# Five changes of order in a gated mix of linear and softmax attention: reciprocals at an iteration's end, weight splits moved, spare banks taken on another turn, the end of the maxima behind its visit, finished sums copied by two engines

## The chip, the cores and the metric

The kernel runs on one core of a Trainium2 chip. The core's engines work side by side: TensorE (PE, with its weight loads shown apart as PEld) multiplies matrices, VectorE (DVE) and ScalarE (ACT) read TensorE's results from the PSUM banks and work element by element, GpSimd (POOL) works from SBUF, and SyncE (SP) issues the transfers (DMA). Every engine runs its own instructions in order and waits on semaphores for the others. The metric is the device time of one execution in microseconds (us); less is better.

## The reference

Two attentions over the same 2048 tokens (448 features, 16 heads of 28) are mixed by a gate per token. Cut to what is computed:

```python
# branch A: linear attention with the Hedgehog feature map
q, k, v = split(x @ A_wqkv)                      # per head: 2048 x 28
phi = lambda u: concat(softmax(u @ w_phi), softmax(-(u @ w_phi)))   # 28 -> 56
kv, z = phi(k).T @ v, phi(k).sum(over tokens)
a = concat_heads((phi(q) @ kv) / (phi(q) @ z + 1e-6)) @ A_wo
# branch B: softmax attention over all keys
q, k, v = split(x @ B_wqkv)
b = concat_heads(softmax(q @ k.T * 28**-0.5) @ v) @ B_wo
g = sigmoid((x * gate_w).sum(-1))
out = g * a + (1 - g) * b
```

Everything is float32. The kernel keeps that precision with a cheaper matmul type (fp32r): an operand is split into a high part (a cast, mostly on ACT) and a low part (the difference, a subtraction on DVE or GpSimd), and a product is made of three passes, high by high, high by low, low by high.

## The kernel before

The heads go in 4 groups of 4, the tokens in 16 tiles of 128 or in 4 query blocks of 512. The order of the instructions on PE, DVE, ACT and GpSimd is the order in which the program writes them; for SP's queue of transfers a scheduler chooses the order. The program has three loops.

**Loop 1 (n below 20)** projects branch B's queries and keys (`proj_qk`, PSUM tiles `pqk`), which go to HBM (qkd), and splits weights: `split_part` casts one half of a weight at once on ACT and queues the subtraction in a list `lows`; `take_lows()` issues what is in the list on DVE.

**Loop 2 (i below 43; q = i - 16, y = q - 1, tb = y // 2)** is branch A with branch B's value projection behind it. The features of keys and queries are made (`features1`, `features2`), `turn` transposes them (`pft`, copied by ACT to `fT`), and `numer(tb)` multiplies them with the summed keys and values (`pn`, two banks). Such a sum then takes four steps, two tiles tb apart, for 8 blocks named a0 to a7:

- `normalize1` copies the two banks to `oUa` on ACT (L362) and has SP gather the denominators (dena).
- `normalize2` adds 1e-6 and inverts on DVE (L371, L372); SP stores the reciprocals to HBM (rda) and loads them back broadcast over partitions (rsa, L377).
- `normalize3` multiplies `oUa` by `rsa` on DVE (L383).
- `normalize4` splits the product into high and low (`oTa`) for the output projection (`poa`, `out_a`).

In the body of loop 2 `normalize2` of block tb - 2 stands after `normalize3` and ahead of the value projection, the weight splits, `numer`, `turn`, `out_a` and the score units. The weights wvB (branch B's values) are split in two halves, at q 14 and 16; `value_b` (tiles `pvb`) uses them at the end of the loop and after it.

Branch B's softmax needs the maximum of each row of scores ahead of the exponentials. The maxima are worked out over the whole program as filler between other matmuls. In loops 1 and 2 and after them `mx_unit` does it 76 times: four matmuls into two pairs of banks (`pmb`, `pmd`, L267), a relu on ACT (L270) and two reductions on DVE (L272) into `part`. In loop 3 `mx_visit` does the rest: up to three score tiles `pm` (three banks, one buffer, L303) and one large reduction on DVE (L311). When a block of queries is complete, `mx_reduce` puts a function into the list `fin`: three small DVE operations that end the maxima. `mx_fin()` runs them at the start of the next unit or visit, and SP then loads the negated maxima into the query tile `qst`.

**Loop 3 (s below 272)** is the softmax attention. Step s (group and query block s // 16, key tile s % 16) makes two score tiles of two banks each (`scores`, `st`, L795), each followed by an exponential on ACT (L797, tile `p`); then `values(s - 1)` adds p times v into one bank `pv` (L898); then `mx_visit` follows. When 16 key tiles are done, `finish` runs `normalize1` with n = 1: here DVE copies the whole of `pv` to `oUb` (L362), and the other three steps follow 3, 8 and 9 steps later. For the last group of heads the output projection (`project`, `pob`, L912) comes from 10 steps after, one tile a step.

The score tiles take turns on two buffers of two banks (`ps2`). Once the maxima are all visited their three banks are free: two of them become a third score buffer, the spare, and one the bank of `pob`:

```python
def ps_p(nm, last=False):
    if spare and spare[0] is not None and not last:
        turns["n"] += 1
        if turns["n"] % 3 == 1:
            return spare[0].tile([P, 2, 512], F32, tag="p", name=nm, bufs=1)
    return ps2.tile([P, 2, 512], F32, tag="p", name=nm, bufs=2)
```

The last sum is finished apart (`finish_last`), with matmuls of the output projection as filler.

Of the kernel before, what the change touches and what calls it, by code (L numbers as in the profile page):

```python
# [19 lines left out]
D = 448  # L20
# [19 lines left out]
def gated_mix_kernel(ctx, tc, xT, wqkB, wvB, wvA, wkAT, wqAT, phi, woA, woB,  # L40
# [7 lines left out]
    nc = tc.nc  # L48
# [106 lines left out]
    mxs = {"u": 0, "f": 0, "fin": []}  # L155
# [55 lines left out]
    def mx_fin():  # L211
        while mxs["fin"]:
            mxs["fin"].pop(0)()
# [72 lines left out]

    def mx_visit():

        mx_fin()
        f = mxs["f"]  # L290
        todo = flats[f:f + 3]
        todo = [x for i, x in enumerate(todo) if x[4] == todo[0][4] + i]
        if not todo:
            return
        mxs["f"] = f + len(todo)
        pm = psm.tile([P, 3, 512], F32, tag="mx", name=f"pm{f}", bufs=1)
        for i, (gq, kb, qt, j, col) in enumerate(todo):
            g, qb = divmod(gq, NQ)
            if kb == 1 and qt in (0, QM) and j == 0 and gq + 1 < NG * NQ:
                if ("qc", gq + 1) not in mxs:  # L300
                    mx_query(gq + 1)
            js = slice(32 * j, 32 * j + DH)
            nc.tensor.matmul(pm[:, i, :], mxs[("qc", gq)][js, qt * P:(qt + 1) * P],  # L303
                             mxs[("kc", g, kb)][js, :], start=True, stop=True,
                             tile_position=(32 * j, 0))
            if j == 3 and qt == 3 and qb == NQ - 1 and g + 1 < NG:
                mx_load(g + 1, kb)
            if kb == 3 and qt == 3 and j == 3:
                mx_reduce(gq)
        n, col = len(todo), todo[0][4]  # L310
        nc.vector.tensor_reduce(part[:, col:col + n], pm[:, :n], AX.X, ALU.max)  # L311


    bd_s = ExitStack()
# [43 lines left out]
    def normalize1(pool, pn, nm, n):  # L358

        oU = pool.tile([P, n, 512], F32, tag="oU", name=f"oU{nm}", bufs=1 + n)  # L360
        for i in range(n):
            (nc.scalar.copy if n == 2 else nc.vector.tensor_copy)(oU[:, i, :], pn[i])  # L362
        den = pool.tile([P, n, 16], F32, tag="den", name=f"den{nm}", bufs=2)
        for i in range(n):
            nc.sync.dma_start(den[:, i, :], oU[DH:P:32, i, :])
        return oU, den
# [64 lines left out]
    fk, va, fq, fT_of, num, oTs = {}, {}, {}, {}, {}, {}  # L431
# [110 lines left out]
    wvA_s = weights(3, "wvA_s")  # L542
# [19 lines left out]
    def split_part(w, key, n, i, low=nc.vector):  # L562
        split_weight(w, raws[key][i], slice(2 * i, 2 * i + 2), slice(0, n), low)
# [16 lines left out]
    for n in range(NP):  # L580
        take_acts()
        if n in (0, 4, 8):
            x_loads(n // 4 + 1)
        if n == 5:
            nc.sync.dma_start(phi_s, phi)
            load_fold(wkAT, "k")
        if n == 10:
            part_loads("wB1", wqkB[:, :, 512:896], 384, "wB1")
        splits(n + 1)
        if n == 14:  # L590
            part_loads("wvA", wvA, 450, "wvA")
            nc.sync.dma_start(sel_s, sel)
            nc.sync.dma_start(mask_s, mask)
            for v in vap:
                nc.gpsimd.memset(v[:, :, 28:32], 0.0)
                nc.gpsimd.memset(v[:, :, 28:29], 1.0)
        if 16 <= n < 20:
            mx_unit()
        proj_qk(n, ev)
        if n in (17, 18):  # L600
            split_part(wvA_s, "wvA", 450, n - 17)
            take_lows()
        if n == 0:
            pkv = ps_pv("pkv")
        if n in (10, 12, 14, 17):
            fold(wkA_s, "k", {10: 0, 12: 1, 14: 2, 17: 3}[n])
        if n == 10:
            pair_query(0, 0)
            pair_load(0, 0)
        if n == 15:  # L610
            pair_load(0, 1)
            pair_query(0, 1)
        if n in (14, 19):
            take_subs()
# [27 lines left out]
    for i in range(2 * NT + 11):  # L642
        t, q = i, i - NT
        y = q - 1
        tb = y // 2
        take_acts()
        if t < NT and t % 2 == 0:
            mx_unit()
            passes = (55 if t < NT - 4 else 44) + (4 if t >= 4 else 0)
            pace["n"], pace["at"] = 4 if t >= 4 else 0, [k * passes // 4 for k in (1, 2, 3)]  # L650
        if q in (0, 1):
            take_exps()

        if t % 2 == 0 and 0 <= t - 4 < NT:
            kv_add(t - 4)
            kv_add(t - 3)
        if q == 2:
            bk_s.close()
            ta_s = ExitStack()
            ta = ta_s.enter_context(tc.tile_pool(name="ta", bufs=1, reuse_waits="tile"))  # L660
            stg = ta_s.enter_context(tc.tile_pool(name="stg", bufs=2, reuse_waits="tile"))
            KV = ta.tile([112, 8, 64], F32, name="KV")
            kvT = kv_copy()
            ps_s_.close()
            ps = ps_s_.enter_context(tc.tile_pool(name="psq", bufs=1, space=PSUM, reuse_waits="tile"))
            psn[0] = 4
            woA_s = weights(3, "woA_s")
            wvB_s = weights(2, "wvB_s")
            take_exps()
        if t < NT:  # L670
            pk = ps_s(f"pk{t}")
            tok_major(pk, t, wkA_s, D, tick)
            fk[t] = features1(pk, f"k{t}", nc.gpsimd)
            take_exps(1)
        if 0 <= q < NT:
            pq = ps_s(f"pq{q}")
            tok_major(pq, q, wqA_s, D)
        if q == 0:
            fk[NT - 1] = features2(fk[NT - 1], f"k{NT - 1}")
        if q in (1, 2):  # L680
            fq[q - 1] = features2(fq[q - 1], f"q{q - 1}")
        if 0 <= q < NT:
            fq[q] = features1(pq, f"q{q}", nc.vector if 0 < q < 9 else nc.gpsimd)
        if 0 <= t - 1 < NT - 1:
            fk[t - 1] = features2(fk[t - 1], f"k{t - 1}")
        if q in (0, 1) or q >= 8:
            mx_unit()
        if y >= 9 and y % 2 and tb - 4 < 8:
            oTs[tb - 4] = normalize4(ta, num.pop(tb - 4), f"a{tb - 4}", 2)
        if q > 0:  # L690
            take_exps(int(q < NT))
        if q == 3:
            kv_out(kvT)
        if 2 <= q - 1 < NT:
            fq[q - 1] = features2(fq[q - 1], f"q{q - 1}")
        take_subs()
        if t == 1:
            pair_load(0, 3)
        if y >= 8 and y % 2 == 0 and tb - 4 < 8:
            num[tb - 4] = normalize3(*num[tb - 4], 2)  # L700
        if y >= 5 and y % 2 and tb - 2 < 8:
            num[tb - 2] = normalize2(ta, *num[tb - 2], f"a{tb - 2}", 2, True)
        if t < NT:
            value_a(t)
            if t % 2 and t < NT - 4:
                proj_qk(NP + t // 2, ev)
        if q in (0, 1):
            proj_qk(NP + 6 + q, ev)
        take_lows()
        if 2 <= i < 4:  # L710
            fold(wqA_s, "q", i - 2, 0, 2)
            fold(wqA_s, "q", i - 2, 2, 2)
        elif 4 <= i < 6:
            fold(wqA_s, "q", i - 2)
        if q == 1:
            ev_s.close()
        if q == 2:
            part_loads("woA", woA, D, "woA")
        if q == 11:
            part_loads("wvB", wvB, D, "wvB")  # L720
        if q in (4, 6):
            split_part(woA_s, "woA", D, (q - 4) // 2)
        if q in (14, 16):
            split_part(wvB_s, "wvB", D, (q - 14) // 2)
        if q == 1:
            gates()
        if y >= 4 and y % 2 == 0 and tb - 2 < 8:
            numer(tb - 2)
        if y < 9 or y % 2:
            if y >= 2 and y - 2 < NT:  # L730
                turn(y - 2)
        if 0 <= y - 10 < NT:
            out_a(y - 10)
            out_a2(y - 10)
        if y >= 9 and y % 2 == 0 and y - 2 < NT:
            turn(y - 2)
        if NT + 3 <= q < NT + 10:
            mx_unit()
        if q == NT + 2:
            bd_s.close()  # L740
            vb = [value_tile(0)]
        if 0 <= q - NT - 2 < 8:
            value_b(q - NT - 2)
    ta_s.close()
    wp_s.close()
    vb.append(value_tile(1))
# [86 lines left out]
    turns = {"n": 0}  # L833
# [6 lines left out]
    def ps_p(nm, last=False):  # L840
        if spare and spare[0] is not None and not last:
            turns["n"] += 1
            if turns["n"] % 3 == 1:
                return spare[0].tile([P, 2, 512], F32, tag="p", name=nm, bufs=1)
        return ps2.tile([P, 2, 512], F32, tag="p", name=nm, bufs=2)

# [280 lines left out]
```

## Time and profile before

| | us |
|---|---|
| time, median of 3 runs (lowest, highest) | 1064.24 (1063.4, 1065.44) |
| profiled execution, its own time | 1062.24 |
| its span in the trace | 1060.4 |
| PE busy | 1043.4 (98%) |
| ACT busy | 723.3 (68%) |
| DVE busy | 706.6 (67%) |
| PE weight loads busy | 567.0 (53%) |
| GpSimd busy | 227.2 (21%) |

The span runs from the first to the last instruction of the profile; the execution's own time holds 1.8 us around it. A timeline row gives the start in us from the span's start, the mean duration, the engine, the line, the operation, the tiles written and read, their shapes and, behind x, how many like it follow each other; a bracket tells how long the engine had been idle and what it waited for. A row of the list of waits gives the engine that waited, what it wanted to do, whom it waited for, the total, the count and the longest. The granted TensorE clock is 1.0 over the whole span.

### The profile page before, as it was taken

What the parts mean: (1) busy time and instruction counts of PE and PEld (TensorE: products, weight loads), DVE (VectorE), ACT (ScalarE), POOL (GpSimd) and SP (SyncE); (2) the same over time, 40 slices, a digit from 0 to 9 for tenths busy, and PEclk for the clock granted to TensorE, in tenths of its full rate; (3) what the DMA queues carried; (4) which work ended last, traced back from release to release, by engine and by line L of the source; (5) the groups of instructions that cost most, each with busy time, mean ns of one, the idle gap of its engine ahead of it and who ended that gap; (6) DMA issues with size and microseconds to landing.
All of it is one profiled execution on the core that took longest, in us unless ns stands there. A gap on an engine that the chain in (4) does not pass through costs nothing.

```text
span 1060.4 us, 16523 instructions
## 1 busy us (share of the span) xinstructions
PE 1043.4 (98%) x6328; PEld 567.0 (53%) x6328; DVE 706.6 (67%) x871; ACT 723.3 (68%) x864; POOL 227.2 (21%) x188
## 2 busy tenths in 40 slices
PE   7999999999999999999999999999999999999998
PEld 5878777878767634344344344343343343454445
DVE  4666776897745567767677777677677777676302
ACT  4455555577755677887777777777777777747572
POOL 0234454678525600120000000000000000000000
PEclk9999999999999999999999999999999999999999
DMA  8873110122232832232533224432233344142311
GB/s 281 293 237 102 37 42 30 40 68 88 88 102 83 184 78 52 53 76 75 119 73 71 72 61 144 111 69 71 63 69 82 76 111 101 46 123 53 101 58 53
DMA packets 65687, 99.03 MB, mean 93 GB/s; under 512 B 17976, under 2 KB 26792, under 8 KB 65608
## 3 DMA queue, kind: packets, MB, share of 16 engines
q1 hardware_dynamic: 65608, 97.97, 33.8%
q8 instruction: 50, 0.82, 0.3%
q14 instruction: 29, 0.24, 0.1%
HBM read 69.77 MB, written 27.78 MB: 92 GB/s over the span
## 4 chain that ended last, share of the span: by engine, by line
PE 93%; DVE 4%; DMA 1%; ACT 1%; issue 0%; POOL 0%; SPq 0%; DVEq 0%; ACTq 0%
PE st L795 27%; PE pv L898 24%; PE pm L303 10%; PE pqk L108 7%; PE pk L126 4%; PE poa L108 3%; PE pva L126 3%; PE pob L108 3%; PE pmb L267 3%; PE pvb L126 2%; PE pq L108 2%; PE pvb L108 1%; PE pn L496 1%; DMA dena<-oUa 1%; PE pft L484 1%; DVE featq L411 1%
## 5 line engine op out<-in xcount | busy, mean ns | idle before, releaser
L797 ACT ACTIVATE p<-st 128x1024 f32<-128x1024 f32 x512 | 496.5, 1021 | 173.4 <-PE st L795 171.9
L311 DVE TENSOR_REDUCE part<-pm 128x3 f32<-128x1536 f32 (+1 forms) x241 | 421.7, 1750 | 167.7 <-PE pm L303 167.4
L795 PE MATMUL st<-qst,kst 128*128 128x512 f32 x1024 | 306.4, 421 | 1.5 <-DVE part L311 1.5
L898 PE MATMUL pv<-p,vb 128*32 128x512 f32 x2048 | 272.8, 605 | 0.0
L795 PEld LDWEIGHTS st<-qst,kst 128*128 128x128 f32 x1024 | 172.9, 188 | 94.1 <-issue 68.2
L303 PEld LDWEIGHTS pm<-kc,qc 28*128 28x128 f32 x720 | 45.4, 182 | 200.1 <-DVE part L311 184.9
L272 DVE CUSTOM_DVE_ANT_0 rl<-pmb,rl 128x512 f32<-128x512 f32 x152 | 98.1, 683 | 56.9 <-ACT rl L270 56.8
L383 POOL TENSOR_TENSOR oUb<-oUb,rsb 128x512 f32<-128x512 f32 x15 | 19.3, 1286 | 521.2 <-DMA rsb<-rdb 326.0
L303 PE MATMUL pm<-kc,qc 28*128 28x512 f32 x720 | 121.4, 497 | 0.5 <-DVE part L311 0.5
L270 ACT ACTIVATE rl<-pmd 128x1024 f32<-128x1024 f32 x76 | 78.1, 1028 | 42.0 <-PE pmd L267 34.4
L898 PEld LDWEIGHTS pv<-p,vb 128*32 128x32 f32 x2048 | 40.4, 108 | 92.9 <-issue 92.2
L108 PE MATMUL pqk<-XH,wB 128*128 128x512 f32 x224 | 70.9, 407 | 6.7 <-ACT XH L327 6.7
L108 PEld LDWEIGHTS pqk<-XH,wB 128*128 128x128 f32 x224 | 42.1, 193 | 17.4 <-ACT XH L327 6.9
L531 ACT CAST ev<-pqk 128x512 fp32r<-128x512 f32 x28 | 16.4, 586 | 43.0 <-PE pqk L108 39.4
L108 PE MATMUL poa<-woA_s,oTa 128*128 128x448 f32 x192 | 43.4, 375 | 0.0
L267 PE MATMUL pmd<-kp,qp 28*128 28x512 f32 x152 | 37.9, 494 | 3.3 <-DVE part L272 3.3
L126 PE MATMUL pk<-wkA_s,XH 128*128 128x448 f32 x128 | 39.4, 382 | 0.0
L532 DVE TENSOR_TENSOR ev<-pqk,ev 128x512 fp32r<-128x512 f32 x28 | 19.3, 691 | 29.7 <-ACT ev L531 29.6
L108 PEld LDWEIGHTS poa<-woA_s,oTa 128*128 128x128 f32 x192 | 34.9, 189 | 6.2 <-issue 3.3
L267 PE MATMUL pmb<-kp,qp 28*128 28x512 f32 x152 | 38.0, 496 | 0.0
L126 PE MATMUL pva<-wvA_s,XH 128*128 128x450 f32 x128 | 37.8, 371 | 0.0
L108 PE MATMUL pq<-wqA_s,XH 128*128 128x448 f32 x128 | 37.4, 374 | 0.2 <-ACT oUa L362 0.2
(135 smaller groups left out, 1038.9 us busy)
## 6 DMA issues: line engine op xcount, KB each, us to landing
qkd<-ev SPq DMA_DIRECT2D x28, 512.0 KB
qst<-qkd SPq DMA_DIRECT2D x64, 224.0 KB
kst<-qkd SPq DMA_DIRECT2D x64, 224.0 KB
od<-oTb SPq DMA_DIRECT2D x48, 112.0 KB
xraw<-in_xT_dram SPq DMA_DIRECT2D x8, 512.0 KB
rsa<-rda SPq DMA_DIRECT2D x8, 512.0 KB
rsb<-rdb SPq DMA_DIRECT2D x15, 256.0 KB
gad<-ga SPq DMA_DIRECT2D x16, 224.0 KB
```

Of the source, the lines that this page charges most:

```text
L108: nc.tensor.matmul(dst, l, r, start=i == 0, stop=i == len(todo) - 1)
L126: nc.tensor.matmul(dst[:, :n], l, r, start=i == 0, stop=i == len(todo) - 1, skip_group_check=True)
L267: nc.tensor.matmul((pb if j < 2 else pd)[:, j % 2, :], qc[js, qt * P:(qt + 1) * P], kc[js, :], start=True, stop=True, tile_position=(32 * ...
L270: nc.scalar.activation(rl, pd, AF.Relu)
L272: nc.vector.tensor_tensor_reduce(rl[:, i, :], pb[:, i, :], rl[:, i, :], 1.0, LOWEST, ALU.add, ALU.max, part[:, col + i:col + i + 1])
L303: nc.tensor.matmul(pm[:, i, :], mxs[("qc", gq)][js, qt * P:(qt + 1) * P], mxs[("kc", g, kb)][js, :], start=True, stop=True, tile_position= ...
L311: nc.vector.tensor_reduce(part[:, col:col + n], pm[:, :n], AX.X, ALU.max)
L383: (nc.gpsimd if n == 1 else nc.vector).tensor_mul(oU, oU, rs)
L532: nc.vector.tensor_sub(e[:, 1, :], pq, f32(e[:, 0, :]))
L795: nc.tensor.matmul(st[:, jl, :], kst_of[(g, kt // 4)][:, j, (kt % 4) * P:(kt % 4 + 1) * P], qst_of[gq][:, j, :], start=True, stop=True)
L797: nc.scalar.activation(p, st, AF.Exp, scale=SCALE)
L898: nc.tensor.matmul(pv[32 * j:32 * j + 32, :], vb[kt // 8][:, kt % 8, 4 * g + j, :], pt[j // 2][:, j % 2, :], start=kt == 0, stop=kt == NT ...
```

## The change

It has five parts.

1. In loop 2 `normalize2` moves from the middle of the iteration to its end, behind value projection, weight splits, `numer`, `turn`, `out_a`, the late score units and `value_b`.
2. The first half of wvA is split at n = 16 instead of 17 (the second stays at 18), and the second half of wvB at q = 17 instead of 16 (the first stays at 14).
3. The score tiles take the spare banks on every third turn as before, but the first of them is the third score tile behind the opening instead of the first.
4. `mx_visit` takes the functions of `fin` out of the list at its start and runs them behind its own large reduction instead of ahead of its matmuls.
5. In `normalize1` with n = 1 DVE copies columns 0 to 383 of `pv`, and ACT copies columns 384 to 511. With n = 2 ACT copies both banks as before.

```diff
     def mx_visit():
-        mx_fin()
+        fins = mxs["fin"][:]
+        mxs["fin"].clear()
         f = mxs["f"]
         todo = flats[f:f + 3]
         todo = [x for i, x in enumerate(todo) if x[4] == todo[0][4] + i]
         if not todo:
+            for fn in fins:
+                fn()
             return
...
         nc.vector.tensor_reduce(part[:, col:col + n], pm[:, :n], AX.X, ALU.max)
+        for fn in fins:
+            fn()
...
     def normalize1(pool, pn, nm, n):
         oU = pool.tile([P, n, 512], F32, tag="oU", name=f"oU{nm}", bufs=1 + n)
-        for i in range(n):
-            (nc.scalar.copy if n == 2 else nc.vector.tensor_copy)(oU[:, i, :], pn[i])
+        for i in range(2):
+            if n == 2:
+                nc.scalar.copy(oU[:, i, :], pn[i])
+            else:
+                c = slice(384 * i, 384 + 128 * i)
+                (nc.scalar.copy if i else nc.vector.tensor_copy)(oU[:, 0, c], pn[0][:, c])
...
-        if n in (17, 18):
-            split_part(wvA_s, "wvA", 450, n - 17)
+        if n in (16, 18):
+            split_part(wvA_s, "wvA", 450, (n - 16) // 2)
             take_lows()
...
-        if y >= 5 and y % 2 and tb - 2 < 8:
-            num[tb - 2] = normalize2(ta, *num[tb - 2], f"a{tb - 2}", 2, True)
         if t < NT:
             value_a(t)
...
-        if q in (14, 16):
-            split_part(wvB_s, "wvB", D, (q - 14) // 2)
+        if q in (14, 17):
+            split_part(wvB_s, "wvB", D, (q - 14) // 3)
...
         if 0 <= q - NT - 2 < 8:
             value_b(q - NT - 2)
+        if y >= 5 and y % 2 and tb - 2 < 8:
+            num[tb - 2] = normalize2(ta, *num[tb - 2], f"a{tb - 2}", 2, True)
...
-            if turns["n"] % 3 == 1:
+            if turns["n"] % 3 == 0:
                 return spare[0].tile([P, 2, 512], F32, tag="p", name=nm, bufs=1)
```

## The prediction, made before the result was known

> **What bounds the kernel now.** I read the page first (busy shares and the chain that ended last), then the list of TensorE's waits, then the timeline around each wait, and at last the spacing of the attention loop.
>
> ```profile
> PE 1043.4 (98%) x6328; PEld 567.0 (53%) x6328; DVE 706.6 (67%) x871; ACT 723.3 (68%) x864; POOL 227.2 (21%) x188
> ...
> PE 93%; DVE 4%; DMA 1%; ACT 1%; issue 0%; POOL 0%; SPq 0%; DVEq 0%; ACTq 0%
> ```
> ```profile
> PE pqk L108 <- ACT XH L327: 6.7, 1, 6.7
> PE pmd L267 <- DVE part L272: 3.3, 3, 2.6
> PE st L795 <- DVE part L311: 1.5, 1, 1.5
> ...
> PE pn L496 <- ACT fT L487: 0.6, 1, 0.6
> PE pm L303 <- DVE part L311: 0.5, 1, 0.5
> ```
>
> TensorE is busy or issuing nearly all the time; DVE and ACT are a third idle. The order of TensorE's instructions is the same in both kernels, so the change can only pay where TensorE waits. Outside the first wait (6.7, the start, untouched) the list holds little: 3.3, 1.5, 0.6 and 0.5 us. I take the parts of the change by the stall that each of them touches, and add waits too short for that list, which show as idle time before weight loads.
>
> **Denominators inverted at an iteration's end.** `normalize2` issues on DVE an add and a reciprocal, on SP two stores (rda) and a broadcast load (rsa). In built order its DVE pair moves past other DVE work in one of the eight cases only, the last: past the two reductions of the score unit that stands late in that iteration.
>
> ```profile
> 300.89 0.50 PE L267 MATMUL pmb<-kp,qp 28*128 28x512 f32 x2
> ...
> 301.53 1.02 ACT L270 ACTIVATE rl<-pmd 128x1024 f32<-128x1024 f32 x1
> ...
> 303.76 0.50 PE L267 MATMUL pmb<-kp,qp 28*128 28x512 f32 x2
> ...
> 304.49 0.80 DVE L371 TENSOR_SCALAR dena<-dena 128x32 f32<-128x32 f32 x1 [3.71 <-DMA dena<-oUa]
> 305.33 0.35 DVE L372 RECIPROCAL dena<-dena 128x32 f32<-128x32 f32 x1
> 305.60 0.63 DVE L272 CUSTOM_DVE_ANT_0 rl<-pmb,rl 128x512 f32<-128x512 f32 x1
> ...
> 306.90 0.50 PE L267 MATMUL pmd<-kp,qp 28*128 28x512 f32 x2 [2.64 <-DVE part L272]
> ```
>
> DVE stands 3.71 us at the add because the denominators have not landed; behind it queue the reductions of the unit of 300.89, and the next unit's pmd needs their bank, so TensorE loses 2.64. Moved ahead, these reductions start at the relu's end, 301.53 + 1.02 = 302.55, and two of some 0.65 each end at 303.9, when the pmd wants to start (some 0.2 after 303.76). At most 0.1 stays: I take 2.6 off. The add still waits until 304.49 and the pair ends at 305.68; behind it now queue the reductions of the unit of 303.76, whose relu ends about 305.6, so they lose 0.1 and the next unit is 3 us off. What is late next is the broadcast:
>
> ```profile
> 294.44 0.56 SPq L377 DMA_DIRECT2D rsa<-rda  x1
> ...
> 308.37 0.56 SPq L377 DMA_DIRECT2D rsa<-rda  x1
> ...
> 322.11 1.22 DVE L383 TENSOR_TENSOR oUa<-oUa,rsa 128x1024 f32<-128x1024 f32 x1
> ```
>
> On SP the stores move behind the row store (gad) and the key loads kp and kt; I allow 0.5 us, so rsa goes out at 308.9. Its use at 322.11 comes some 3.2 earlier, 318.9: 10 us. The denominators queued behind the rsa of 294.44 had landed by 304.49, so a broadcast takes under 10. It just fits; lateness could give back up to 1 us. Ends for this part: 1.3 to 2.7, taken 2.6 since only rows of exact order enter it. In the seven other cases the pair keeps its place on DVE; only SP's order shifts by a DMA, in an iteration whose multiply comes three iterations later: nothing.
>
> **Weight splits moved.** wvB's second half is cast on ACT and subtracted on DVE one iteration later.
>
> ```profile
> 276.75 0.95 ACT L142 CAST wvB_s<-wvB_raw 128x896 fp32r<-128x896 f32 x1
> ...
> 277.58 1.09 ACT L487 COPY fT<-pft 112x512 f32<-112x512 f32 x2
> ...
> 278.24 1.95 PE L496 MATMUL pn<-fT,KV 112*64 112x256 f32 x16 [0.60 <-ACT fT L487]
> ```
>
> With the cast gone from ahead of them the two fT copies start at 276.8 and the 0.60 goes. The cast lands behind the next relu, ahead of the two oUa copies, which end 0.3 later than now; nobody asks for their banks before the next transposes at 282: hidden. The subtraction lands behind the reductions that end about 286.7:
>
> ```profile
> 272.81 2.58 DVE L143 TENSOR_TENSOR wvB_s<-wvB_raw,wvB_s 128x896 fp32r<-128x896 f32 x1
> ...
> 282.87 1.08 DVE L143 TENSOR_TENSOR wvB_s<-wvB_raw,wvB_s 128x896 fp32r<-128x896 f32 x1
> ...
> 286.04 2.54 POOL L392 TENSOR_TENSOR oTa<-oUa,oTa 128x512 fp32r<-128x512 f32 x2 [5.82 <-ACT oTa L391]
> ...
> 286.71 0.66 DVE L371 TENSOR_SCALAR dena<-dena 128x32 f32<-128x32 f32 x1
> ...
> 287.26 0.40 PEld L108 LDWEIGHTS pvb<-wvB_s,XH 128*128 128x128 f32 x2
> ```
>
> Its place is now the add's of 286.71, beside two GpSimd passes of 1.27 each. The add got in between them (286.04 + 1.27 = 287.31, end 287.37). The subtraction would run 287.31 to 288.39. TensorE reads this low half in the eighth matmul of the tile begun at 287.26, at 0.2 a matmul 288.7: 0.3 to spare. The GpSimd pass held up by 1.08 feeds matmuls three us off. So 0.6 off, from -0.4 (below, second rival) to 0.6. wvA's first half is cast one projection earlier; three pmd waits make 3.3 and 2.64 is spent, so at most 0.7 can be gained there, and the reductions pushed back 1.1 could lose 0.1. Taken 0.
>
> **Spare banks first used later.**
>
> ```profile
> 986.31 0.68 DVE L912 SCALAR_TENSOR_TENSOR acc<-pob,gate,acc 128x448 f32<-128x448 f32 x1 [0.68 <-PE pob L108]
> 986.91 1.22 DVE L311 TENSOR_REDUCE part<-pm 128x2 f32<-128x1024 f32 x1
> ...
> 988.18 0.76 PEld L795 LDWEIGHTS st<-qst,kst 128*128 128x128 f32 x4 [1.79 <-DVE part L311]
> ...
> 1042.65 0.30 PEld L795 LDWEIGHTS st<-qst,kst 128*128 128x128 f32 x2 [0.40 <-ACT p L797]
> ```
>
> The spare tile lies in the banks of the maxima, so the first score tile on it waits for the last maxima reduction (986.91 + 1.22). With the new turn that tile takes a bank of the old pair; its second waits for the projection's reader, done at 986.99, within 0.1 of when it is wanted. TensorE's 1.5 goes; the projection after it, behind eight value matmuls, starts past 988.2 and does not wait. The turn also shifts the end: the last two score tiles use the old pair, which before the change had just served the two tiles ahead, hence 0.40 before a weight load at 1042.65; now the one ahead is on the spare. Regular loads there follow without gap, and the step loses about 0.25: off.
>
> **End of maxima behind its visit.**
>
> ```profile
> 934.52 1.72 DVE L311 TENSOR_REDUCE part<-pm 128x3 f32<-128x1536 f32 x1
> ...
> 936.29 0.51 PE L303 MATMUL pm<-kc,qc 28*128 28x512 f32 x3 [0.50 <-DVE part L311]
> ```
>
> The end (three small DVE operations, 0.64) stands ahead of a visit's large reduction, which frees the bank for the next visit. Mostly it fits into DVE's 0.8 idle per step; beside a projection it does not, and 0.50 is lost once. Behind the reduction it fits: 0.5 off. The negated maxima come some 2 us later for SP's loads into the query tile, which is used over 10 us later: nothing.
>
> **Finished sums in two parts.**
>
> ```profile
> L362 ACT COPY oUa<-pn x16: 566/588/659, 213.9 to 292.2; 128x512 f32<-128x512 f32 x16
> L362 DVE COPY oUb<-pv x15: 691/691/692, 407.5 to 1003.5; 128x512 f32<-128x512 f32 x15
> ```
> ```profile
> 491.89 0.19 PEld L303 LDWEIGHTS pm<-kc,qc 28*128 28x128 f32 x3 [0.90 <-DVE part L311]
> ...
> 571.50 0.69 DVE L362 COPY oUb<-pv 128x512 f32<-128x512 f32 x1 [0.44 <-PE pv L898]
> 572.11 1.75 DVE L311 TENSOR_REDUCE part<-pm 128x3 f32<-128x1536 f32 x1
> ...
> 572.56 1.94 ACT L797 ACTIVATE p<-st 128x1024 f32<-128x1024 f32 x2 [0.60 <-PE st L795]
> ...
> 954.89 0.19 PEld L303 LDWEIGHTS pm<-kc,qc 28*128 28x128 f32 x3 [0.91 <-DVE part L311]
> ```
>
> After a copy the next visit's load idles 0.90 instead of the regular 0.84: 0.06 late, 12 times between the first and last row. DVE's part shrinks by a quarter, at 691 ns for 512 columns about 0.13 less: the 0.06 goes, 0.7 in all. ACT's quarter is 15 new instructions. By 566 ns for 512 columns it lies between 0.14 and 0.57; near 0.25, as a short copy keeps a fixed share. As built it waits for DVE's part, so it starts at about 572.1 and ends at 572.4, before the exponential of 572.56. The Trainium skill, "PSUM — Partial Sum Buffer", section "PSUM bank collisions raise a hardware error", says why the halves can't overlap: two engines may not read one bank in the same partitions at once. No run here shows the error; by the page's rule the sum freed is later than by overlap, and its next user, at 572.85, still does not wait. At the last copy, near 1003.5, ACT has less idle time; I charge 0.05.
>
> **Sum.** 2.6 + 0.6 + 1.5 + 0.25 + 0.5 + 0.7 - 0.05 = 6.1 us. The profiled execution took 1062.24 (span 1060.4) and would take 1056.1 (span 1054.3). The median of the runs shown is 1064.24, 2.0 above it; less 6.1 that is 1058.1, my prediction.
>
> **Rivals.** *The stall at the denominators moves on.* If they land later than at 304.49, the next unit's reductions are held as these were, or the last broadcast misses its multiply. For it: DVE stays in order and 3.7 us of lateness are real; against: 3 us lie between units. Half the 2.6 would stay: 1059.4. Chance 0.12.
>
> *The low half of wvB comes late.* If both GpSimd passes go first, it runs 288.58 to 289.66, 1.0 after it is read: 1059.1. The row of 286.71 speaks against it, 272.81 (2.58 for 1.08) for it. The Trainium skill, "SBUF — State Buffer", section "SBUF: two separate sides", calls the port pair of the two engines an exclusive lock for a whole instruction; the 2.58 agrees. Chance 0.13.
>
> *Slower: ACT's part holds up the exponentials.*
>
> ```profile
> 506.21 1.94 ACT L797 ACTIVATE p<-st 128x1024 f32<-128x1024 f32 x2 [0.91 <-PE st L795]
> ...
> 508.20 0.30 PEld L795 LDWEIGHTS st<-qst,kst 128*128 128x128 f32 x2 [0.26 <-ACT p L797]
> ```
>
> An exponential 0.3 late (0.91 idle for 0.62) made the next scores wait 0.26, of which 0.1 reached the following step. So lateness beyond 0.2 counts in full. ACT's part of length p is late by p - 0.45; with p = 0.66, the longest copy above, 0.21: nothing. Against the other 5.4 us, 15 finishes turn the kernel slower by 2.1 only beyond 0.5 each, p = 1.15, more than twice its upper price: then 1066.3. No row shows so short an ACT copy, so the chance is 0.06.
>
> *No effect:* the stalls are followed by others and under 2.1 us remains: about 1063. Chance 0.10.
>
> **Numbers.** Forecast 0.59, at 1056.5 to 1060: no wait can give more than the 6.1 + 0.7 of wvA plus some 0.8 of spread between runs, and the small terms may fail together. With the two partial rivals, both still faster, the range is 1056.2 to 1061.8. A measurement tells about 0.2% (2.1 us) from no change: faster 0.84, same 0.10, slower 0.06.
>
> **What would show it.** TensorE's waits should hold no 2.6 at pmd, no 1.5 at st, no 0.6 at pn, no 0.5 at pm; loads after a copy idle 0.84; ACT copies of some 0.25 right behind DVE's. Wrong would be: a new wait of pvb for wvB, of DVE for rsa about 318, or of st for late exponentials after each copy.

## The result, and the profile after

The changed kernel takes 1056.73 us in the median of its first four executions (1055.75 to 1057.58), the kernel before 1064.84; the ratio is 0.993, 95% interval 0.9912 to 0.9948. In a second comparison, with 6 executions against 29, the medians are 1056.65 and 1063.96 and the ratio is 0.9942 (0.9928 to 0.9956), which is 6.2 us (4.7 to 7.7). The two medians by themselves lie 7.3 us apart, and 8.1 in the first comparison. The forecast was 6.1 us and 1058.1.

The page of the changed kernel, busy shares and the chain that ended last:

```profile
PE 1043.1 (99%) x6328; PEld 566.3 (54%) x6328; DVE 705.1 (67%) x871; ACT 726.8 (69%) x879; POOL 227.7 (22%) x188
...
PE 93%; DVE 4%; POOL 1%; ACT 0%; DMA 0%; issue 0%; SPq 0%; DVEq 0%; ACTq 0%; POOLq 0%
```

TensorE is as busy as before, in a span of 1055.8 us for 1060.4. Its list of waits:

```profile
PE pqk L108 <- ACT XH L332: 6.7, 1, 6.7
PE pmd L267 <- DVE part L272: 0.7, 2, 0.5
PE pft L493 <- ACT fT L496: 0.6, 1, 0.6
PE pm L306 <- DVE part L314: 0.5, 1, 0.5
PE pd L990 <- DVE oUlast L986: 0.2, 1, 0.2
```

The 2.6 at pmd, the 1.5 at st and the 0.6 at pn are gone. The list still holds 0.5 at pm, but at another step (see part 4 alone), and a wait for the last sum (oUlast) is new.

The order of TensorE's instructions is the same in all these kernels, so the start of each matmul can be set against the start of the same matmul before. By how many us a stretch of the kernel before (its bounds in us) became shorter in the traces:

| kernel | 270–300 | 300–310 | 310–860 | 860–960 | 960–1000 | 1000–end |
|---|---|---|---|---|---|---|
| changed | 0.63 | 2.95 | 0.35 | 0.19 | 1.60 | -0.38 |
| changed, second trace | 0.63 | 2.96 | 0.32 | 0.58 | 1.54 | -0.35 |
| part 1 alone | -0.02 | 2.97 | 0.16 | 0.04 | -1.50 | -0.02 |
| part 2 alone | -0.18 | -0.04 | 0.13 | 0.06 | -1.55 | -0.01 |
| part 3 alone | 0.00 | -2.71 | 0.26 | 0.04 | 1.55 | 0.00 |
| part 4 alone | 0.00 | 1.33 | -0.07 | 0.56 | -1.51 | -0.03 |
| part 5 alone | -0.04 | 1.31 | 0.36 | 0.14 | -1.53 | -0.37 |
| parts 1 and 3 | -0.04 | 2.95 | 0.12 | 0.06 | 1.60 | 0.00 |

The first 270 us are left out: their length differs by up to 4 us from that of the kernel before, and only the moved half of wvA touches them (see part 2 alone). The changed kernel's rows add up to 5.3 and 5.7 us. What stands in one column for several kernels that don't hold the part (-1.5 at 960–1000, -2.71 at 300–310) is the main finding below. The 1.3 at 300–310 of parts 4 and 5 alone is something else: in those two executions the stall there was only 1.3 us long.

### The profile page after: what moved, and what is told of

Read it like the earlier page. It is cut to its first block, busy times and chain, and to the rows that moved or that the text cites. A ratio compares the mean times of both kernels' runs of the same rounds, so it can differ in the third digit from the quotient of the medians.

```text
span 1055.8 us, 16548 instructions
## 1 busy us (share of the span) xinstructions
PE 1043.1 (99%) x6328; PEld 566.3 (54%) x6328; DVE 705.1 (67%) x871; ACT 726.8 (69%) x879; POOL 227.7 (22%) x188
## 4 chain that ended last, share of the span: by engine, by line
PE 93%; DVE 4%; POOL 1%; ACT 0%; DMA 0%; issue 0%; SPq 0%; DVEq 0%; ACTq 0%; POOLq 0%
PE st L804 27%; PE pv L907 24%; PE pm L306 10%; PE pqk L108 7%; PE poa L108 4%; PE pk L126 4%; PE pva L126 3%; PE pmb L267 3%; PE pob L108 3%; PE pvb L126 2%; PE pvb L108 2%; PE pq L108 1%; PE pn L505 1%; PE pft L493 1%; DVE featq L420 1%; DVE fsumq L429 1%
```

## The experiments

**The whole change again.**

> The changed kernel once more, in five rounds, to see how large its gain is. If the gain is the sum of the stalls that the two traces show apart from their first 44 us (0.6 at pn, 2.9 at pmd, 0.7 after the copies, 0.5 at step 221, 1.5 at the spare, less 0.6 at step 202 and 0.3 at the end: 5.3 us), the time is 5 to 6 us below the kernel before. If the change does more than these stalls show, as the medians of the first comparison say (1064.84 to 1056.73), it is 8 us below.

1056.65 us (1056.13 to 1057.58). By the ratio this is 6.2 us (4.7 to 7.7) below the kernel before, nearer to the sum of the stalls; by the medians it is 7.3, nearer to 8. So this run doesn't decide between the two answers. What is over the 5.3 to 5.7 of the table is taken up at parts 1 and 3 together.

**Part 1 alone.**

```diff
-        if y >= 5 and y % 2 and tb - 2 < 8:
-            num[tb - 2] = normalize2(ta, *num[tb - 2], f"a{tb - 2}", 2, True)
...
             value_b(q - NT - 2)
+        if y >= 5 and y % 2 and tb - 2 < 8:
+            num[tb - 2] = normalize2(ta, *num[tb - 2], f"a{tb - 2}", 2, True)
```

> Only the denominators' inversion moved to the iteration's end. My step: the 2.64 us wait of pmd is gone, nothing takes its place, 2.6 to 2.9 us faster. Rival, the stall moves on to the next unit's reductions or to the broadcast: a wait of 1 us or more at pmd or at the multiply on DVE about 319 us, 1.3 us faster.

1060.59 us (1059.11 to 1064.25) against 1063.96, ratio 0.9974 (0.9958 to 0.9989). In its trace 2.97 us are gone between 300 and 310. The mechanism is seen best in the timeline of the changed kernel:

```profile
302.68 0.69 DVE L272 CUSTOM_DVE_ANT_0 rl<-pmb,rl 128x512 f32<-128x512 f32 x1 [1.81 <-ACT rl L270]
...
304.05 0.50 PE L267 MATMUL pmd<-kp,qp 28*128 28x512 f32 x2
304.37 1.05 DVE L380 TENSOR_SCALAR dena<-dena 128x32 f32<-128x32 f32 x1 [0.38 <-DMA dena<-oUa]
...
308.83 0.54 SPq L386 DMA_DIRECT2D rsa<-rda  x1
...
319.24 1.22 DVE L392 TENSOR_TENSOR oUa<-oUa,rsa 128x1024 f32<-128x1024 f32 x1
```

The reductions run at 302.68 while the denominators are still under way, pmd follows without a wait, and DVE idles 0.38 at the add, not 3.71. The broadcast leaves at 308.83 (forecast 308.9) and its multiplication runs at 319.24 (forecast 318.9) without waiting. The stall did not move on.

**Part 3 alone.**

```diff
-            if turns["n"] % 3 == 1:
+            if turns["n"] % 3 == 0:
```

> Only the turn of the spare banks. My step: the 1.5 us wait of st at 988 is gone, 1.5 us faster. At the end I had forecast 0.25 more, since the last score tile but one should sit on other banks; the trace of the changed kernel shows the same 0.40 ahead of a weight load at 1037.65, so I now expect 0.40 there again. Rival: the wait turns up at the projection or at the second spare tile, under 0.5 us faster.

1061.66 us (1058.42 to 1065.78) against 1063.96, ratio 0.9981 (0.9966 to 0.9997); 1.55 us gone between 960 and 1000, nothing at the end. But its stretch from 300 to 310, which the part doesn't touch, became 2.71 us longer. The rows below give the busy time of each engine in a stretch of 5 us; the last column but two is the granted clock. First part 3 alone behind the stall at pmd, then, in the window of the other stall, part 1 alone, the kernel before and the changed kernel:

```profile
306.00:311.00 5.00, 2.37 (x9) 1.26 (x8) 2.67 (x6) 1.09 (x2) 1.84 (x2) 0.81 0.17 56
```
```profile
985.00:990.00 5.00, 4.66 (x17) 2.67 (x18) 0.94 (x4) 1.94 (x2) 0.00 (x0) 0.69 0.13 47
```
```profile
985.00:990.00 5.00, 3.52 (x21) 1.84 (x19) 3.10 (x6) 0.99 (x2) 0.00 (x0) 1.00 0.12 46
```
```profile
985.00:990.00 5.00, 5.00 (x29) 3.19 (x25) 1.09 (x4) 2.60 (x4) 0.00 (x0) 1.00 0.14 50
```

Behind a stall the granted clock can fall to a half: for 3.4 us in the traces of parts 1, 2, 4 and 5 alone (each behind the 1.5 us stall at 988), for 6.8 us behind the 2.6 us stall in that of part 3 alone. The matmuls after it then run at half the pace, and the stretch loses another 1.5 or 2.7 us. It does not happen each time: the trace of the kernel before has both stalls and keeps the clock at 1.00. Over the six traces with such stalls there are 12 waits of 1 us or more behind the start, and 7 of them are followed by a half clock. The length alone doesn't decide it: a wait of 2.69 at pmd in the trace of part 2 alone was not followed by it, one of 1.03 in that of part 3 alone was.

**Parts 1 and 3 together.** The edits of both.

> Inversion at the iteration's end and the turn of the spare banks together, nothing else: the two long stalls of TensorE (2.64 at pmd, 1.5 at st) are both gone. Theory of the clock (in the run of part 1 alone the granted clock fell to a half for 3.4 us around the 1.5 us stall, in that of part 3 alone for 6.8 us around the 2.6 us stall, and not in other executions): without stalls of over 1 us no execution loses more, so the times of this kernel lie within 3 us of each other, while the kernel before spreads over 9 us, and the median gains more than the 4.4 us of the two waits, 5 to 6. Rival, the spread comes from elsewhere (the loads at the start): it stays at 5 to 9 us and the gain is 4.4.

1057.98 us in 11 executions, all between 1057.37 and 1058.73, against 1063.48 (1061.16 to 1070.84 in 22); ratio 0.9947 (0.9931 to 0.9962), 5.5 us. The spread is 1.4 us where it is 9.7 in the kernel before, 5.1 with part 1 alone and 7.4 with part 3 alone. So it is the two stalls together that make the spread, as the theory of the clock says and the rival doesn't.

The mean granted clock is on record for every execution, and it shows more than the traces. A half clock for 3.4 us takes 0.0016 off the mean of 1060 us. The 77 executions of the kernel before whose clock is on record:

| mean granted clock | executions | median us (lowest, highest) |
|---|---|---|
| 1.000 | 7 | 1061.16 (1060.42, 1062.81) |
| 0.998 | 39 | 1062.96 (1061.55, 1065.87) |
| 0.996 or 0.997 | 24 | 1064.88 (1063.87, 1066.99) |
| 0.995 or 0.993 | 7 | 1068.51 (1066.12, 1070.84) |

So the expectation's "not in other executions" was wrong: in 70 of 77 executions the clock fell, and each step down goes with 1.8 us or more. The profiled execution of the kernel before was one of the few that kept it. All 50 executions of kernels with both parts read 0.999 or 1.000. Against the seven executions at 1.000 the changed kernel (1056.65) is 4.5 us faster, against all by the medians 7.3; whether these seven also had a shorter stall at pmd the record doesn't show.

The removal of the two stalls shortens the trace by 2.95 + 1.60 = 4.55 us; the rest up to 5.5 fits the clock losses saved, though the interval of this run (4.0 to 7.3 us) doesn't exclude 4.55. The traces of parts 3 and 4 alone hold another half clock of 3.4 us, from 66.7 on, behind waits of pmd of 1.0 and 1.4 us; what they hang on is seen at part 2 alone.

**Part 2 alone.**

```diff
-        if n in (17, 18):
-            split_part(wvA_s, "wvA", 450, n - 17)
+        if n in (16, 18):
+            split_part(wvA_s, "wvA", 450, (n - 16) // 2)
...
-        if q in (14, 16):
-            split_part(wvB_s, "wvB", D, (q - 14) // 2)
+        if q in (14, 17):
+            split_part(wvB_s, "wvB", D, (q - 14) // 3)
```

> Only the moved weight splits. My step: the 0.60 us wait of pn for the copy fT is gone and no wait of pvb comes, the stretch from 270 to 300 us is 0.6 shorter; the moved half of wvA changes nothing by itself. Rival, the low half of wvB comes behind both GpSimd passes: a wait of up to 1 us at pvb.

1062.91 us against 1064.07, ratio 0.999 (0.9977 to 1.0003): within what can be told. In the trace the matmuls win 0.67 at pn, where 0.60 had been a wait, and lose 0.81 at pvb, where 0.55 is a wait now; so the rival happened here. The timeline of part 2 alone, then that of the whole change:

```profile
286.36 2.55 POOL L392 TENSOR_TENSOR oTa<-oUa,oTa 128x512 fp32r<-128x512 f32 x2 [5.18 <-ACT oTa L391]
...
287.03 0.67 DVE L371 TENSOR_SCALAR dena<-dena 128x32 f32<-128x32 f32 x1
...
288.00 1.86 DVE L143 TENSOR_TENSOR wvB_s<-wvB_raw,wvB_s 128x896 fp32r<-128x896 f32 x1
...
289.91 0.47 PE L108 MATMUL pvb<-wvB_s,XH 128*128 128x448 f32 x1 [0.55 <-DVE wvB_s L143]
```
```profile
286.10 3.39 POOL L401 TENSOR_TENSOR oTa<-oUa,oTa 128x512 fp32r<-128x512 f32 x2 [5.14 <-ACT oTa L400]
...
286.77 1.57 DVE L143 TENSOR_TENSOR wvB_s<-wvB_raw,wvB_s 128x896 fp32r<-128x896 f32 x1
...
288.26 1.72 DVE L380 TENSOR_SCALAR dena<-dena 128x32 f32<-128x32 f32 x1
```

Alone, the add and the reciprocal of the denominators stand ahead of the subtraction, and it ends at 289.86. With part 1 they stand behind it: it gets in between the two GpSimd passes, ends at 288.34, and nothing waits. The moved half of wvB pays only with part 1.

The moved half of wvA, which by the expectation changes nothing by itself, does touch a wait. Its subtraction and the pmd of about 65 us, in part 4 alone (half at n = 17), then in the changed kernel (n = 16):

```profile
61.64 2.17 DVE L143 TENSOR_TENSOR wvA_s<-wvA_raw,wvA_s 128x900 fp32r<-128x900 f32 x1
...
65.61 0.50 PE L267 MATMUL pmd<-kp,qp 28*128 28x512 f32 x2 [1.36 <-DVE part L272]
```
```profile
58.64 1.10 DVE L143 TENSOR_TENSOR wvA_s<-wvA_raw,wvA_s 128x900 fp32r<-128x900 f32 x1 [0.15 <-ACT wvA_s L142]
...
64.67 0.50 PE L267 MATMUL pmd<-kp,qp 28*128 28x512 f32 x2
```

At n = 17 the subtraction stands ahead of the reductions that this pmd needs. In the six traces of such kernels the pmd waits 0.6 to 1.4 us in four (parts 1, 3, 4 and 5 alone) and not in two; in the eight traces with n = 16 it never waits, and the next pmd, at 68, waits at most 0.35. The two longest of these waits are the ones with the half clock from 66.7 on. What this is worth in the median no run here shows.

**Part 4 alone.**

```diff
-        mx_fin()
+        fins = mxs["fin"][:]
+        mxs["fin"].clear()
...
         nc.vector.tensor_reduce(part[:, col:col + n], pm[:, :n], AX.X, ALU.max)
+        for fn in fins:
+            fn()
```

> Only the end of the maxima behind its visit. My step: the 0.5 us wait of pm at step 221 is gone. In two traces of the changed kernel 0.58 and 0.16 are lost at step 202 instead, where the negation stands beside a GpSimd multiplication. If part 4 brings that loss by itself, step 202 takes more than 2.6 here too and nothing is won; if it needs the denominators of part 5, step 202 takes 2.56 and 0.5 is won. In the median at most 0.5 either way.

1062.45 us against 1063.48, ratio 0.999 (0.9972 to 1.0009). (Steps 27, 57, 86, 175, 202 and 221 are counted from one, so the program's s is one less.) In the trace the 0.5 at step 221 is won and step 202 costs nothing, although the negation there takes 0.59, not 0.17. In the changed kernel's first trace it cost 0.58:

```profile
875.39 1.29 POOL L392 TENSOR_TENSOR oUb<-oUb,rsb 128x512 f32<-128x512 f32 x1 [35.74 <-ACT p L806]
875.49 1.22 DVE L236 TENSOR_SCALAR neg<-red 128x16 fp32r<-128x16 f32 x1
...
876.88 1.72 DVE L314 TENSOR_REDUCE part<-pm 128x3 f32<-128x1536 f32 x1
...
878.65 0.51 PE L306 MATMUL pm<-kc,qc 28*128 28x512 f32 x3 [0.51 <-DVE part L314]
```

The negation of 128x16 numbers stands still until the GpSimd multiplication ends, and holds the next visit's large reduction. The multiplication starts when its broadcast lands, so the two meet by chance: in the eight traces with part 4 the negation at this place took 0.51 to 1.22 in seven and 0.17 in one (ACT copies all, below), and in the six without part 4 always 0.17. Part 4 moves this negation back by 2.4 us, into that neighbourhood.

**Another form for the negation.**

```diff
-            nc.vector.tensor_scalar_mul(neg[:, :16], red, -1.0)
+            nc.vector.scalar_tensor_tensor(neg[:, :16], red, -1.0, f32(neg[:, 16:32]),
+                                           op0=ALU.mult, op1=ALU.add)
```

> The changed kernel, but the negation of the maxima is made with the three-operand form (times -1, plus a row of zeros) in place of the two-operand one. About 116 us the negation took 1.8 us beside a GpSimd pass in every run so far, and 1.2 us at step 202 in the trace of the changed kernel, against 0.17 elsewhere. If only some forms of DVE's instructions wait for GpSimd, and this one doesn't, its longest falls below 0.4 us and step 202 takes 2.56. If this form waits too, its longest stays at 1.8. In the median at most 0.5 us either way.

1056.63 us (ratio to the kernel before 0.9932, 0.9907 to 0.9958), no difference from the changed kernel. The 1.8 us case stands at 338 us, not at 116 as the expectation has it. First the changed kernel (its second trace), then the other form, at that place and at step 202:

```profile
337.87 1.81 POOL L765 MEMSET qst<- 128x2048 f32 x1 [2.33 <-PE poa L108]
337.89 1.81 DVE L236 TENSOR_SCALAR neg<-red 128x16 fp32r<-128x16 f32 x1
```
```profile
337.13 1.81 POOL L766 MEMSET qst<- 128x2048 f32 x1 [2.38 <-PE poa L108]
337.15 0.18 DVE L236 SCALAR_TENSOR_TENSOR neg<-red,neg 128x16 fp32r<-128x16 f32 x1
...
874.39 1.29 POOL L393 TENSOR_TENSOR oUb<-oUb,rsb 128x512 f32<-128x512 f32 x1 [35.58 <-DMA rsb<-rdb]
874.64 1.07 DVE L236 SCALAR_TENSOR_TENSOR neg<-red,neg 128x16 fp32r<-128x16 f32 x1
```

So neither answer was whole: the three-operand form passes a GpSimd memset, and is held by a GpSimd multiplication. The Trainium skill, "SBUF — State Buffer", section "SBUF: two separate sides", says this: the port pair is locked by DVE instructions in a 2-port mode, or with two SBUF inputs, the latter only against a GpSimd instruction that reads SBUF. The four rows agree with it, if the two-operand form runs in such a mode.

**Part 5 alone.**

```diff
-        for i in range(n):
-            (nc.scalar.copy if n == 2 else nc.vector.tensor_copy)(oU[:, i, :], pn[i])
+        for i in range(2):
+            if n == 2:
+                nc.scalar.copy(oU[:, i, :], pn[i])
+            else:
+                c = slice(384 * i, 384 + 128 * i)
+                (nc.scalar.copy if i else nc.vector.tensor_copy)(oU[:, 0, c], pn[0][:, c])
```

> Only the copies in two parts. My step: 12 copies cost TensorE 0.06 us less each, 0.7 us faster, 15 ACT copies of 0.27 us start where DVE's part ends. Rival, ACT's part delays the exponential behind it: score loads that wait for ACT after each copy, same time or slower.

1064.32 us against 1063.96, ratio 1.0011 (0.9999 to 1.0024): no gain. The groups of copies and one copy with its neighbours, in the changed kernel:

```profile
L371 DVE COPY oUb<-pv x15: 557/558/559, 404.7 to 998.5; 128x384 f32<-128x384 f32 x15
L371 ACT COPY oUb<-pv x15: 266/266/267, 405.3 to 999.1; 128x128 f32<-128x128 f32 x15
```
```profile
568.59 0.56 DVE L371 COPY oUb<-pv 128x384 f32<-128x384 f32 x1 [0.44 <-PE pv L907]
569.06 1.75 DVE L314 TENSOR_REDUCE part<-pm 128x3 f32<-128x1536 f32 x1
569.18 0.27 ACT L371 COPY oUb<-pv 128x128 f32<-128x128 f32 x1
569.64 1.94 ACT L806 ACTIVATE p<-st 128x1024 f32<-128x1024 f32 x2 [0.20 <-PE st L804]
570.92 0.19 PEld L306 LDWEIGHTS pm<-kc,qc 28*128 28x128 f32 x3 [0.84 <-DVE part L314]
```

The mechanism is as forecast: ACT's part takes 0.27, begins where DVE's ends, the exponential behind it still has 0.20 to spare, and the load behind the copy idles the regular 0.84. The twelve losses of 0.06 are gone. But two other delays came with the part. At the end the copy of the last sum starts 0.37 later, and three steps (27, 86, 175) are 0.09 longer where it was one before (57):

```profile
577.61 1.02 ACT L806 ACTIVATE p<-st 128x1024 f32<-128x1024 f32 x1 [0.90 <-PE st L804]
...
1041.68 0.69 DVE L986 COPY oUlast<-pv 128x512 f32<-128x512 f32 x1 [5.86 <-PE pv L907]
...
1042.43 1.05 PE L990 MATMUL pd<-sel_s,oUlast 128*128 128x4 f32 x8 [0.24 <-DVE oUlast L986]
```

The exponential of 577.61 idles 0.90 where 0.62 is regular, as the one of 506.21 did in the kernel before. In neither row does a semaphore come late.

**Who copies: ACT all, or DVE both parts.**

```diff
-                (nc.scalar.copy if i else nc.vector.tensor_copy)(oU[:, 0, c], pn[0][:, c])
+                if i:
+                    nc.scalar.copy(oU[:, 0, :], pn[0])
```
```diff
-                (nc.scalar.copy if i else nc.vector.tensor_copy)(oU[:, 0, c], pn[0][:, c])
+                nc.vector.tensor_copy(oU[:, 0, c], pn[0][:, c])
```

> The changed kernel, but ACT copies the whole 512 columns of a finished sum and DVE nothing. By the rows, ACT's copy takes 0.57 to 0.6 and makes the exponential behind it 0.1 to 0.2 late; by my slower rival's own rule lateness below 0.2 costs nothing, so the copies cost TensorE nothing: 0 to 0.4 us faster than the changed kernel. If lateness counts from the first tenth on, each of 12 copies costs 0.1 to 0.15 and the time is 1 to 2 us above it. DVE has 15 instructions less, so its copy of the last sum, 0.37 late with part 5, may start on time again if that lateness hangs on where DVE's instruction stream is loaded.

> The changed kernel, but DVE copies the second part too, right behind the first. By the rows two parts take 0.56 + 0.27 = 0.83 on DVE, 0.14 more than one copy of 0.69, so the loads behind a copy idle 0.2 longer than regular and not 0.06: 12 copies cost 2.4 us, against 0 with ACT's part: 2 us slower than the changed kernel. Rival: DVE's idle 0.8 a step takes it, no difference. DVE has 15 instructions more, so the copy of the last sum, 0.37 late in each run with part 5 as written and on time where ACT copies all, should be on time if its lateness hangs on where DVE's instruction stream is loaded.

ACT all: 1055.99 us (1055.23 to 1056.98). DVE both: 1058.56 (1057.55 to 1059.6). Against the second trace of the changed kernel, ACT all costs nothing in the loop (310 to 960 changes by under 0.4 in its favour) and DVE both loses 1.7 between 364 and 960, near the 2 forecast. In both the copy of the last sum is on time again, 0.35 earlier; here with DVE both parts:

```profile
L372 ACT COPY oUb<-pv x15: 593/597/597, 404.1 to 997.4; 128x512 f32<-128x512 f32 x15
```
```profile
1042.22 0.69 DVE L986 COPY oUlast<-pv 128x512 f32<-128x512 f32 x1 [5.49 <-PE pv L907]
```

ACT's whole copy takes 0.60, its quarter 0.27, and the scores lose nothing by it.

Counted over the traces, with the semaphore instructions that the page leaves out, the last copy is DVE's 960th instruction in the five traces where it is late (part 5 alone, the changed kernel twice, the other form of the negation, the last score tiles), and the 935th, 961st, 962nd or 975th in those where it is on time. The late exponentials go the same way: steps 27, 86 and 175 where ACT has 1575 instructions, step 57 where it has 1548.

The late exponentials are ACT's 576th, 832nd and 1216th instruction in the first case and its 704th in the second. Each of these counts, 960 too, is 64 above a multiple of 128; the 512th and 640th of the changed kernel, multiples of 128, start after the regular 0.62 and 0.63. (Not every such place shows a delay: several fall where ACT doesn't idle.) So these delays hang on a place in the engine's stream and not on the copy. At the same places the trace of the changed kernel holds transfers of 8 KB of the kind "instruction": at 427.5, 578.3, 807.3 and 1042.3 us one begins, 0.6 to 1.9 behind the late start. Where ACT copies all, DVE has only 953 instructions, and one such transfer less is made (28 for 29 on their queue). That the engine changes over to another loaded block there would explain the delay; no run here shows directly what it waits for.

**The last score tiles.**

```diff
-            st = ps_p(f"st{s}_{i}", s == NS - 1)
+            st = ps_p(f"st{s}_{i}", s == NS - 1 and i == 1)
```

> The changed kernel, but the last but one score tile may also take the spare banks, so that the last one finds banks that have been free for a while. If the 0.40 ahead of the last score load is a wait for the banks of the tile two before it, as I read it, it goes and the end comes 0.25 to 0.4 earlier. Rival: the first projection of the end needs the spare banks at once and waits for them, no gain or up to 0.5 slower.

1055.81 us (1055.6 to 1056.68). Weight loads of the last scores, changed kernel and this one:

```profile
1036.95 0.30 PEld L804 LDWEIGHTS st<-qst,kst 128*128 128x128 f32 x2 [0.84 <-ACT p L806]
1037.65 0.30 PEld L804 LDWEIGHTS st<-qst,kst 128*128 128x128 f32 x2 [0.40 <-ACT p L806]
```
```profile
1035.22 0.77 PEld L804 LDWEIGHTS st<-qst,kst 128*128 128x128 f32 x4 [0.84 <-issue]
```

The 0.40 is gone, the four loads run as one row, and the step is 0.2 us shorter. The first projection of the end doesn't wait. The median is 0.84 below that of the changed kernel, which was not run again beside it; of this only 0.2 is shown to come from the edit. In its trace the first 45 us, which the edit doesn't touch, were 0.9 to 1.0 shorter than in the two of the changed kernel.

**A version with all of it.** ACT copies all, the last score tiles as above, and:

```diff
         w, c = wB[m // 4], m % 4 * P
+        if n == 0:
+            for _ in range(16):
+                nc.tensor.matmul(pq[:, :P], ident, ident, start=True, stop=True)
```

> The changed kernel with three edits: ACT copies all 512 columns (the end 0.35 earlier in its own run), the last but one score tile may take the spare banks (0.2 earlier in its own run), and 16 matmuls of the identity by itself, whose result is overwritten, run while TensorE waits 6.8 us for its first operand. In all traces the first 6 to 7 us of real matmuls run at half the clock (0.63 us instead of 0.39 a matmul, about 14 of them, so 0.2 x 14 = 2.8 us at most), and by how much it differs from run to run explains the remaining spread of 1.5 us. If work ahead of them raises the clock earlier, the first 14 us become 1 to 2 us shorter (the operands' own arrivals hold the rest) and the time is 1.5 to 2.5 us below the changed kernel. Rival: matmuls of the identity don't raise it, or they end after the operand is there; then only 0.5 is gained, or up to 1 lost at the start.

1056.08 us (1055.56 to 1057.82), no better than the changed kernel (1056.65) by more than their spread. Its start:

```profile
1.36 5.74 PE L541 MATMUL pqk<-ident 128*128 128x128 f32 x32 [1.36 <-POOL ident masks.py:199]
...
8.54 0.39 PE L108 MATMUL pqk<-XL,wB 128*128 128x512 f32 x1
9.86 0.73 PE L108 MATMUL pqk<-XH,wB 128*128 128x512 f32 x2 [0.93 <-ACT XH L332]
```

The matmuls ahead do raise the clock: the real one at 8.54 takes 0.39, where such a matmul takes 0.63 in the other traces until the clock rises, 10.6 to 13.8 us from their start. (So the granted clock of 1.0 given for the kernel before holds from 12 us on.) But TensorE then waits 0.93 for the second part of XH: the operands' arrival bounds the first 12 us, and nothing is won.

## Why the prediction was right, and where not

*Denominators, 2.6:* right; 2.95 to 2.97 in four traces, 0.3 more, and every later time (304.4, 308.8, 319.2) came within 0.4. In the traces of parts 4 and 5 alone the stall was only 1.3 long: DVE's wait for the denominators and the add together took 3.2 there, not 4.5. The term was sized from one execution.

*Weight splits, 0.6:* right for the whole change, 0.63, with the subtraction between the two GpSimd passes as worked out (288.34, forecast 288.39). What the step didn't say is that this place is free only because part 1 takes the add out of it. Alone, part 2 meets the second rival. The half of wvA, "taken 0", was put at nothing from a trace in which the pmd at 64 didn't wait; in four of six traces without the move it waits 0.6 to 1.4.

*Spare banks, 1.5 + 0.25:* 1.54 to 1.60, right. The 0.25 at the end failed: I counted the turns from one step too late. The first step with the spare is 236, and with turn 3 the tiles of step 254 both take the old pair, so the last score tile still waits for a tile just read. The run that gives it other banks wins the 0.2 by another edit.

*End of maxima, 0.5:* "Behind the reduction it fits" failed. The 0.5 at step 221 is won in the traces of part 4 alone and of the changed kernel, and up to 0.58 is lost at step 202, because the negation there stands beside a GpSimd multiplication. DVE's 0.8 idle per step is right; a 0.17 us instruction isn't 0.17 us there.

*Copies in two parts, 0.7 - 0.05:* ACT's price (0.25, measured 0.27), its start behind DVE's part and the harmless exponential were right. The net term was not: the end lost 0.37 instead of 0.05, and three late exponentials took 0.09 each. Part 5 alone gains nothing that can be measured.

*The sum* of 6.1 lies inside the measured 4.7 to 7.7, in part by luck. The stalls give 5.3 to 5.7 in the traces, less than forecast by the end and by step 202; the stalls of parts 1 and 3 cost more than their length when the clock falls behind them. It fell in 70 of 77 executions of the kernel before, and in none of the 50 with both stalls gone. That second price stood nowhere in the prediction. It took the gain from a profiled execution that had kept its clock and subtracted it from a median whose executions mostly hadn't: against executions at clock 1.000 the gain is 4.5, below the 6.1, and between the medians it is 7.3 or 8.1, above it. The errors in the small terms and the missing clock term balance in part.

*Rivals:* the stall did not move on, ACT's part did not hold up the scores even at 0.60, and the change had its effect. wvB's low half came late only where part 2 stood alone.

## What to carry to other kernels

Where a matmul-bound kernel waits 1 us or more once, look at the granted clock of many executions and not of one trace: the loss can be twice the wait, and the spread of the times shows it before a single trace does. Test the parts of a change alone as well as together: two of the five here (2 and 5) gain nothing that can be told by themselves, and one of these pays only because another part clears its place. A tiny DVE instruction is priced by what GpSimd does at that moment, not by its size.

## What the runs showed of the hardware

- A stall of TensorE of 1.0 to 2.6 us was followed in some executions by half the clock for 3.4 us (once 6.8), at a cost of 1.5 to 2.7 us on top of the wait; in 70 of 77 executions of the kernel before the mean granted clock was below 1.000. The Trainium skill, "TensorE: Matmul & The Clock Gate", section "Part 1: The HAM clock gate (the "warmup" mystery)", gives windows of about 3.4 us and a fall after an idle window of that length; the 3.4 agrees, but here waits of 1.0 to 1.5 us were enough. Whether the load of the whole window counts is not shown.
- DVE's two-operand negation waited 1.81 us for a GpSimd memset; its three-operand form passed the memset in 0.18 and waited 1.07 for a GpSimd multiplication.
- An engine can start 0.28 to 0.37 us late with no semaphore outstanding, at a place that moves when instructions are added or removed ahead of it: in these traces at counts of its instructions 64 above a multiple of 128.
